# Attention and FFN on one core: strided value tiles of 128 rows, strided pairs first, masks loaded in two parts

## The chip, the core and the metric

The kernel runs on one core of one Trainium2 chip. The metric is the device time of one execution in microseconds (us), the median of several. The engines named below are PE (TensorE matmul; PEld is its weight load), DVE (VectorE), ACT (ScalarE), POOL (GpSimd) and SP (SyncE, which here only issues DMAs). The core has 16 DMA engines.

## What is computed

Eight batches of eight heads, 576 tokens, head size 64. Heads 0 to 3 see a local window of the last 32 tokens, heads 4 to 7 see every 32nd token back from their own. The result goes, token by token, through an FFN of 512 to 2048 to 512.

```python
def reference(q, k, v, w_in, w_out):
    scores = q @ k.T / sqrt(64)                  # per batch and head
    rel = i - j
    mask = (0 <= rel < 32) if head < 4 else (rel >= 0 and i % 32 == j % 32)
    attn = softmax(where(mask, scores, -1e9)) @ v
    x = attn.transpose(0, 2, 1, 3).reshape(4608, 512)
    h = x @ w_in
    return (h * sigmoid(1.702 * h)) @ w_out
```

## The kernel before, in words

The host lays the inputs out in the order in which the kernel reads them (`_layout`, from L707). Attention is cut into units, called pairs in the code. A *local* pair ("l") holds four blocks of 64 queries with 96 keys each, for four heads: its queries and keys come in one tile of 128 rows (`qk <- lqk`, 576 KB), its values in one of 96 rows (`v <- lv`, 384 KB). A *strided* pair ("s") holds a third of a batch's 32 residue classes: `qk <- sqk`, 452 KB in 128 rows, and its values `v <- sv`, in 118 rows of 2 KB (236 KB; `QB + NB` is 64 + 54: two groups of 54 keys, the second from row 64 on). There are 18 local and 24 strided pairs.

`_pairs` (L59) lists the pairs in the order of the work: `ahead`, those done before the FFN starts, and `windows`, those woven into the FFN of later token groups. A token group is 384 tokens; the FFN of a group takes 16 steps (one for each 128 of the 2048 hidden units), `ffn1` making a hidden tile and `ffn2` adding it, two steps later, to three output tiles. Nine pairs are ahead: before the change l, l, s, s, s, s, l, s, s. They are numbered 0 to 8 below; the stretch in which they are done is called the lead.

The lead is a loop written out by hand (L607 to L635). In iteration i, for a pair each: PE makes the scores of pair i+1 (`scores`: masks are added by a matmul of the mask rows with an identity matrix, both from the tile `masks_sb`, then 32 small matmuls); SP loads the qk of pair i+3; DVE and POOL scale pair i-1 by the reciprocal of its sums; DVE fetches pair i-2's transposed weights from PSUM (`fetch_pt`); DVE takes the row maxima of pair i+1; ACT does the exponentials of pair i (eight instructions); PE makes the value products of pair i-2 (`values`, the matmuls "a <- pt, v"); ACT casts them to the FFN's high part (`xhl`, `xhs`), DVE later makes the low part; SP loads the values of pair i; ACT and DVE do one of the three passes that split a 128-wide slice of the FFN weights (`weigh`, from tiles `raw`) into high and low parts; PE transposes pair i-1 (`turn_pr`, "t"). Each engine keeps to the order in which the program is written.

Two things tie SP's queue to the rest. The qk and v tiles have two buffers each, so `load_qk(i+3)` waits for the scores of pair i+1, and `load_v(i)` for the value products of pair i-2; what stands behind a waiting load on SP waits too. And a DMA that shares its completion semaphore with an earlier one waits until that has landed; eight semaphores go round.

After the lead come the FFN steps, in which PE is kept busy by the `ffn1` and `ffn2` matmuls ("h" and "o"); the strided and local pairs that remain are done beside them, with the mask added on DVE instead. The lead's end and the first steps overlap: the value products of pairs 6, 7 and 8 stand before, in and after steps 0 to 2 on PE, and the weight slices for steps 2 and on are loaded and split while the steps run.

The tile `masks_sb` is 672 columns wide: five local mask blocks of 96, the strided one of 54 at `MASK_S` (480), the identity at `MASK_I` (544). One DMA (L154) loads it first of all. `geom` (L171) picks the mask of a pair, `scores` (L193) the identity.

Of the kernel before, what the change touches and what calls it, by code (L numbers as in the profile page):

```python
# [18 lines left out]
P = 128  # L19
B, H, S, D = 8, 8, 576, 64  # L20
# [4 lines left out]
QB = 64  # L25
KB = QB + STRIDE
RB = 3
NB = RB * NPOS
U = 2
# [3 lines left out]
NR = (12, 10, 10)  # L33
# [1 line left out]
QW = (U * 2 * QB, U * (NB + QB))  # L35
KW = (U * (KB + QB), U * 2 * NB)
QKW = tuple(2 * (a + b) for a, b in zip(QW, KW))
MASK_S = 5 * KB
MASK_I = 544
MASKS = MASK_I + P  # L40
G = 384
NG = B * S // G
NF = DFF // P
# [4 lines left out]
HEADS = 4  # L48
# [10 lines left out]
def _pairs():  # L59

    def strided(b):
        return [("s", b, c) for c in range(len(NR))]

    def local(j):
        return [("l", i, 0) for i in range(-(-j * G // LT), -(-(j + 1) * G // LT))]

    def weave(a, b):
        return [u for i in range(max(len(a), len(b))) for u in a[i : i + 1] + b[i : i + 1]]  # L70

    first = {}
    for b in range(B):
        first.setdefault(b * S // G, []).extend(strided(b))
    ahead = local(0) + first[0]
    windows = [weave(first.get(j + 1, []), local(j + 1)) for j in range(NG - 1)] + [[]]
    ahead += windows[0]
    windows[0] = []
    return ahead + [u for w in windows for u in w], windows, len(ahead)
# [3 lines left out]
def attn_ffn(ctx, tc, lqk, sqk, lv, sv, w_in, w_out, masks, ident, out):  # L83
# [11 lines left out]
    def bank(name):  # L95
        tag, n = ("s", 2) if name[0] == "s" else ("x", 6)
        return psum.tile([P, 512], F32, tag=tag, name=name, bufs=n)
# [8 lines left out]
    class InOrder:  # L106
# [17 lines left out]
    vector, scalar, gpsimd, sync = (  # L124
        InOrder(e, strict) for e in (nc.vector, nc.scalar, nc.gpsimd, nc.sync)
    )
# [3 lines left out]
    qks, vts, banks, nmaxs, exps = {}, {}, {}, {}, {}  # L130

    def load_qk(p):
        if p < len(pairs) and p not in qks:
            kind, a, c = pairs[p]
            src, n = (lqk[a], QKW[0]) if kind == "l" else (sqk[a * len(NR) + c], QKW[1])
            qks[p] = st4([P, QKW[0]], F32, f"qk_{p}")
            for i in (slice(0, n // 2), slice(n // 2, n)) if p == 0 else (slice(0, n),):
                sync.dma_start(out=qks[p][:, i], in_=src[:, i])

    def load_v(p):  # L140
        if p < len(pairs) and p not in vts:
            kind, a, c = pairs[p]
            vts[p] = io.tile([P, 2 * U * HEADS * D], F32, tag="v", name=f"v_{p}", bufs=2)
            if kind == "l":
                sync.dma_start(out=vts[p][:KB], in_=lv[a])
            else:
                n = U * HEADS * D
                sync.dma_start(out=vts[p][: QB + NB, :n], in_=sv[a * len(NR) + c])

    warm = const.tile([P, 1], F32, name="warm")  # L150
    vector.memset(warm, 0.0)
    scalar.activation(warm, warm, AF.Exp)
    masks_sb = const.tile([P, MASKS], BF16, name="masks_sb")
    sync.dma_start(out=masks_sb, in_=masks)  # L154
    load_qk(0)
    zeros = const.tile([P, P], BF16, name="zeros")
    vector.memset(zeros, 0.0)
# [4 lines left out]
    first = [[bank(f"{x}{j}") for j in range(2)] for x in "sut"]  # L162
# [8 lines left out]
    def geom(p):  # L171

        kind, a, _ = pairs[p]
        if kind == "s":
            m = masks_sb[:, MASK_S : MASK_S + NB]
            return NB, m.unsqueeze(1).broadcast_to([P, 2 * U, NB])
        begins = [i for i in range(2 * U) if (2 * U * a + i) % (S // QB) == 0]
        if not begins:
            m = masks_sb[:, KB : 2 * KB]
            return KB, m.unsqueeze(1).broadcast_to([P, 2 * U, KB])  # L180
        at = (0, 2, 3, 1)[begins[0]] * KB
        m = masks_sb[:, at : at + U * KB]
        return KB, m.unsqueeze(1).broadcast_to([P, 2, U * KB])

# [8 lines left out]
    def scores(p):  # L193

        nk, mask = geom(p)
        onto = p < n0
        sps = first[p % 2] if onto else [bank(f"s{j}_{p}") for j in range(2)]
        n = mask.shape[1]
        if onto:
            for sp in sps:  # L200
                matmul(
                    sp[:, : 2 * U * nk].rearrange("p (a n) -> p a n", a=n),
                    lhsT=masks_sb[:, MASK_I:], rhs=mask, start=True, stop=False,
                )
        for h in range(2):
            for u in range(U):
                i = h * U + u
                for g in range(2):
                    for j in range(2):
                        q, k = operands(p, slice(j * D, (j + 1) * D), h, u, g)  # L210
                        matmul(
                            sps[j][g * QB : (g + 1) * QB, i * nk : (i + 1) * nk],
                            lhsT=q,
                            rhs=k,
                            start=not onto,
                            stop=not onto or i == 2 * U - 1,
                        )
        banks[p] = sps
# [169 lines left out]
    def load_w(f):  # L388

        if f >= NF:  # L390
            return
        raw = raws[f] = w_tile([P, 2, DM, 2], U32, f"raw_{f}")
        for m in range(2):
            sync.dma_start(out=raw[:, m], in_=(w_in, w_out)[m][f])
# [190 lines left out]
    for _ in range(6):  # L585
        matmul(
            first[2][0].rearrange("p (a n) -> p a n", a=4), lhsT=zeros,
            rhs=zeros.unsqueeze(1).broadcast_to([P, 4, P]), start=True, stop=True,
# [2 lines left out]
    maxima(0)  # L591
    load_qk(2)
    load_v(1)
    load_w(0)
    halfway, valued = {}, {}

# [41 lines left out]
    at = {}  # L638
# [3 lines left out]
    p = n0  # L642
# [10 lines left out]
    begins = {}  # L653
    for p in range(n0, len(pairs)):
        begins[max(turn.get(p - AHEAD, -1) + 1, turn[p] - SOON)] = p
    for s in range(len(steps) + LAG):
# [3 lines left out]
        p, q, r = due.get(s), due.get(s - 1), begins.get(s)  # L660
# [46 lines left out]
def _layout(q, k, v, w_in, w_out):  # L707
    hl = H // 2
    pad = np.zeros((B, hl, STRIDE, D), np.float32)
    kp, vp = (np.concatenate([pad, x[:, :hl]], axis=2) for x in (k, v))  # L710
    nb = S // QB

    lqk = np.zeros((NP, 2, D, 2, QKW[0] // 2), np.float32)
    lv = np.zeros((NP, KB, 2 * U, HEADS, D), np.float32)
    for i in range(NP):
        for m in range(2 * U):
            b, n = divmod(2 * U * i + m, nb)
            u, g = divmod(m, 2)
            rows = q[b, :hl, n * QB : (n + 1) * QB]
            keys = kp[b, :, n * QB : n * QB + KB]  # L720
            at = u * 2 * QB + g * QB
            lqk[i, :, :, :, at : at + QB] = rows.reshape(2, 2, QB, D).transpose(1, 3, 0, 2)
            at = QW[0] + u * (KB + QB) + g * QB
            skip = STRIDE if g and not n else 0
            lqk[i, :, :, :, at + skip : at + KB] = keys[:, skip:].reshape(
                2, 2, KB - skip, D
            ).transpose(1, 3, 0, 2)
            lv[i, :, m] = vp[b, :, n * QB : n * QB + KB].transpose(1, 0, 2)

    ns = B * len(NR)  # L730
    sqk = np.zeros((ns, 2, D, 2, QKW[1] // 2), np.float32)
    sv = np.zeros((ns, QB + NB, U, HEADS, D), np.float32)
    for i in range(ns):
        b, c = divmod(i, len(NR))
        for m in range(2 * U):
            g, u = divmod(m, U)
            r0, r1 = R0[c] + RB * m, R0[c] + min(RB * (m + 1), NR[c])
            n = (r1 - r0) * NPOS
            x = [
                y[b, hl:].reshape(hl, NPOS, STRIDE, D)[:, :, r0:r1].transpose(0, 2, 1, 3).reshape(hl, n, D)  # L740
                for y in (q, k, v)
            ]
            at = u * (NB + QB) + g * NB
            sqk[i, :, :, :, at : at + n] = x[0].reshape(2, 2, n, D).transpose(1, 3, 0, 2)
            at = QW[1] + u * 2 * NB + g * NB
            sqk[i, :, :, :, at : at + n] = x[1].reshape(2, 2, n, D).transpose(1, 3, 0, 2)
            sv[i, g * QB : g * QB + n, u] = x[2].transpose(1, 0, 2)
    lqk, sqk = (x.reshape(len(x), P, -1) for x in (lqk, sqk))
    lv, sv = (x.reshape(*x.shape[:2], -1) for x in (lv, sv))

    wi = w_in.reshape(NC, P, NF, P).transpose(2, 1, 0, 3).reshape(NF, P, DM)
    wo = w_out.reshape(NF, P, DM)
    wi, wo = (np.ascontiguousarray(x).view(np.uint64) for x in (wi, wo))
    return lqk, sqk, lv, sv, wi, wo


def _masks():
    import ml_dtypes

    m = np.full((P, MASKS), NEG, ml_dtypes.bfloat16)  # L760
    i, g = np.arange(P)[:, None] % QB, np.arange(P)[:, None] // QB
    k = np.arange(KB)[None, :] - STRIDE
    ok = (i - k >= 0) & (i - k < STRIDE)
    for n, begins in enumerate((0, None, 1, None, 0)):
        some = ok if begins is None else ok & ((g != begins) | (k >= 0))
        m[:, n * KB : (n + 1) * KB][some] = 0.0
    k = np.arange(NB)[None, :]
    ok = (i // NPOS == k // NPOS) & (i >= k)
    m[:, MASK_S : MASK_S + NB][ok] = 0.0
    m[:, MASK_I:] = np.eye(P)  # L770
    return m


# [24 lines left out]
```

## Time and profile before

| | |
|---|---|
| three runs | 947.21, 945.47, 946.59 us; median 946.59 |
| the profiled execution | 947.53 us |
| its span, first to last instruction | 945.7 us |
| PE busy | 913.9 us, 97% of the span |
| DVE, ACT, POOL busy | 476.1, 380.6, 53.0 us |
| moved by DMA | 62.08 MB, 66 GB/s over the span |
| mean granted clock of TensorE | 0.98 of full speed |

The profile is one execution on the chip. Its page gives the busy time of each engine; a table by stretches gives it for any piece of the span, with PE's granted clock (1.00 is full speed), the share of the 16 DMA engines that was busy and the GB/s they moved. The time line gives instructions in order: start, duration, engine, line, operation, out<-in, and in brackets the idle time ahead of the first one and what ended it. All engines go through one helper, so every row has the same line, L116, and rows are told apart by their tiles. The chain of waits follows the work that ended last back from the end. A DMA's row on SP is its issue, not its transfer.

### The profile page before, as it was taken

What the parts mean: (1) busy time and instruction counts of PE and PEld (TensorE: products, weight loads), DVE (VectorE), ACT (ScalarE), POOL (GpSimd) and SP (SyncE); (2) the same over time, 40 slices, a digit from 0 to 9 for tenths busy, and PEclk for the clock granted to TensorE, in tenths of its full rate; (3) what the DMA queues carried; (4) which work ended last, traced back from release to release, by engine and by line L of the source; (5) the groups of instructions that cost most, each with busy time, mean ns of one, the idle gap of its engine ahead of it and who ended that gap; (6) DMA issues with size and microseconds to landing.
All of it is one profiled execution on the core that took longest, in us unless ns stands there. A gap on an engine that the chain in (4) does not pass through costs nothing.

```text
span 945.7 us, 16069 instructions
## 1 busy us (share of the span) xinstructions
PE 913.9 (97%) x6432; PEld 806.6 (85%) x6432; DVE 476.1 (50%) x986; ACT 380.6 (40%) x1193; POOL 53.0 (6%) x50
## 2 busy tenths in 40 slices
PE   6569999999999999999999999999999999999998
PEld 4457888888888888888888888888888888898997
DVE  3648656565454663443655564453446565322322
ACT  5649755243433442423444333332433443222221
POOL 3100001010000100000000000000000010000000
PEclk6779999999999999999999999999999999999999
DMA  8659202112112111101212120110201310000000
GB/s 262 197 164 348 97 1 90 60 41 96 35 42 84 53 53 51 45 1 64 72 50 72 52 57 34 53 38 20 80 31 43 105 29 1 34 1 1 34 1 33
DMA packets 21242, 62.08 MB, mean 66 GB/s; under 512 B 2144, under 2 KB 2400, under 8 KB 21168
## 3 DMA queue, kind: packets, MB, share of 16 engines
q1 hardware_dynamic: 21168, 61.06, 19.7%
q8 instruction: 50, 0.82, 0.4%
q14 instruction: 24, 0.20, 0.1%
HBM read 51.62 MB, written 9.44 MB: 65 GB/s over the span
## 4 chain that ended last, share of the span: by engine, by line
PE 92%; DMA 7%; DVE 0%; issue 0%; SPq 0%; ACT 0%; DVEq 0%; ACTq 0%
PE o L116 43%; PE h L116 41%; PE a L116 4%; DMA v<-sv 4%; PE s L116 3%; DMA raw<-w_out 1%; DMA qk<-sqk 1%; DMA qk<-lqk 1%; PE u L116 0%; PE t L116 0%; SPq L116 0%; ACT raw L116 0%; DVE raw L116 0%; DVE w L116 0%; DVE out L116 0%
## 5 line engine op out<-in xcount | busy, mean ns | idle before, releaser
L116 PE MATMUL o<-w,gh 128*128 128x512 f32 x1152 | 307.6, 398 | 0.0
L116 PEld LDWEIGHTS o<-w,gh 128*128 128x128 f32 x1152 | 211.1, 187 | 39.0 <-ACT gh L116 0.4
L116 PE MATMUL h<-xhl,w 128*128 128x384 f32 x768 | 229.7, 339 | 2.0 <-DVE w L116 1.4
L116 PE MATMUL h<-xhs,w 128*128 128x384 f32 x768 | 227.2, 336 | 0.0
L116 DVE SCALAR_TENSOR_TENSOR g<-g,h 128x384 f32<-128x384 f32 x192 | 106.1, 553 | 225.2 <-ACT g L116 224.6
L116 ACT ACTIVATE g<-h 128x384 f32<-128x384 f32 x192 | 93.7, 488 | 264.3 <-PE h L116 188.1
L116 PE MATMUL o<-w,gl 128*128 128x512 f32 x576 | 169.6, 395 | 0.0
L116 ACT CAST gh<-g 128x384 fp32r<-128x384 f32 x192 | 98.8, 514 | 155.2 <-DVE g L116 155.1
L116 PEld LDWEIGHTS h<-xhl,w 128*128 128x128 f32 x768 | 142.3, 188 | 12.2 <-DVE w L116 2.3
L116 DVE TENSOR_TENSOR gl<-g,gh 128x384 fp32r<-128x384 f32 x192 | 112.0, 583 | 77.6 <-ACT gh L116 76.1
L116 PEld LDWEIGHTS h<-xhs,w 128*128 128x128 f32 x768 | 141.9, 188 | 0.1
L116 PEld LDWEIGHTS o<-w,gl 128*128 128x128 f32 x576 | 107.8, 187 | 26.6
L116 PE MATMUL h<-xll,w 128*128 128x384 f32 x384 | 129.6, 338 | 0.0
L116 PE MATMUL h<-xls,w 128*128 128x384 f32 x384 | 128.7, 335 | 0.0
L116 ACT ACTIVATE pr<-pr,nmax 128x54 f32<-128x54 f32 (+1 forms) x264 | 90.3, 344 | 87.6 <-DVE nmax L116 84.6
L116 POOL TENSOR_TENSOR pr<-pr,rinv 128x432 f32<-128x432 f32 (+1 forms) x42 | 49.6, 1182 | 734.5 <-DVE rinv L116 728.0
L116 PEld LDWEIGHTS h<-xll,w 128*128 128x128 f32 x384 | 72.4, 189 | 8.8
L116 PEld LDWEIGHTS h<-xls,w 128*128 128x128 f32 x384 | 72.4, 188 | 0.0
L116 DVE STREAM_TRANSPOSE pt_l<-pr 32x256 f32<-32x256 f32 x120 | 52.2, 435 | 2.3 <-POOL pr L116 0.8
L116 DVE STREAM_TRANSPOSE pt_s<-pr 32x256 f32<-32x256 f32 x108 | 47.1, 436 | 9.5 <-POOL pr L116 8.0
L116 ACT ACTIVATION_READ_ACCUMULATOR pr<-pr,nmax 128x1 f32 x264 | 49.4, 187 | 0.0
L116 PE MATMUL a<-pt_s,v 118*64 118x108 f32 x384 | 25.3, 278 | 13.8 <-DMA v<-sv 12.2
(55 smaller groups left out, 462.3 us busy)
## 6 DMA issues: line engine op xcount, KB each, us to landing
qk<-sqk SPq DMA_DIRECT2D x24, 452.0 KB
qk<-lqk SPq DMA_DIRECT2D x17, 576.0 KB
out<-out SPq DMA_DIRECT2D x36, 256.0 KB
raw<-w_in SPq DMA_DIRECT2D x16, 512.0 KB
raw<-w_out SPq DMA_DIRECT2D x16, 512.0 KB
v<-lv SPq DMA_DIRECT2D x18, 384.0 KB
v<-sv SPq DMA_DIRECT2D x24, 236.0 KB
qk<-lqk SPq DMA_DIRECT2D x2, 288.0 KB
```

The costliest lines, as they stand in the source:

```text
L116: ins = call(*args, **kw)
```

## The change

Three edits, all to what stands around the lead.

*Values in 128 rows.* The host pads the strided values from 118 to 128 rows with zeros, and `load_v` loads all 128 (256 KB). The value products still read 118 rows.

*Strided pairs first.* In `_pairs`, the first group's strided pairs go ahead of its local ones: the nine pairs are now s, s, s, l, l, s, l, s, s. The pairs from the sixth on are the same as before.

*Masks in two parts.* The tile's columns are laid out anew: the strided mask, the identity, then the local blocks from `MASK_L` (192) on. The first DMA loads 192 columns (48 KB), a second one, issued behind the values of pair 1, the other 480 (120 KB).

```diff
-MASK_S = 5 * KB
-MASK_I = 544
-MASKS = MASK_I + P
+MASK_I = 64
+MASK_L = MASK_I + P
+MASKS = MASK_L + 5 * KB
...
-    ahead = local(0) + first[0]
+    ahead = first[0] + local(0)
...
-                sync.dma_start(out=vts[p][: QB + NB, :n], in_=sv[a * len(NR) + c])
+                sync.dma_start(out=vts[p][:, :n], in_=sv[a * len(NR) + c])
...
-    sync.dma_start(out=masks_sb, in_=masks)
+    sync.dma_start(out=masks_sb[:, :MASK_L], in_=masks[:, :MASK_L])
...
-            m = masks_sb[:, MASK_S : MASK_S + NB]
+            m = masks_sb[:, :NB]
...
-            m = masks_sb[:, KB : 2 * KB]
+            m = masks_sb[:, MASK_L + KB : MASK_L + 2 * KB]
...
-        at = (0, 2, 3, 1)[begins[0]] * KB
+        at = MASK_L + (0, 2, 3, 1)[begins[0]] * KB
...
-                    lhsT=masks_sb[:, MASK_I:], rhs=mask, start=True, stop=False,
+                    lhsT=masks_sb[:, MASK_I:MASK_L], rhs=mask, start=True, stop=False,
...
     load_qk(2)
     load_v(1)
+    sync.dma_start(out=masks_sb[:, MASK_L:], in_=masks[:, MASK_L:])
     load_w(0)
...
-    sv = np.zeros((ns, QB + NB, U, HEADS, D), np.float32)
+    sv = np.zeros((ns, P, U, HEADS, D), np.float32)
```

How this moves instructions is read from the built programs, engine by engine. First SP at the start of the program, before: the masks, then the loads of pairs 0 to 4 (`qk_0`, `v_0` and so on are the tiles of pair 0; `raw_0` is the first slice of the FFN weights).

```order
L116 DMA masks_sb_82<-masks 128x672
L116 DMA qk_0_84<-lqk 128x576 x2
L116 DMA qk_1_107<-lqk 128x1152
L116 DMA v_0_109<-lv 96x1024
L116 DMA ident_sb_111<-ident 128x128
L116 DMA qk_2_141<-sqk 128x904
L116 DMA v_1_143<-lv 96x1024
L116 DMA raw_0_145<-w_in 128x1024
L116 DMA raw_0_145<-w_out 128x1024
L116 DMA qk_3_166<-sqk 128x904
L116 DMA qk_4_199<-sqk 128x904
```

The same place now:

```order
L116 DMA masks_sb_82<-masks 128x192
L116 DMA qk_0_84<-sqk 128x452 x2
L116 DMA qk_1_107<-sqk 128x904
L116 DMA v_0_109<-sv 128x512
L116 DMA ident_sb_111<-ident 128x128
L116 DMA qk_2_141<-sqk 128x904
L116 DMA v_1_143<-sv 128x512
L116 DMA masks_sb_82<-masks 128x480
L116 DMA raw_0_146<-w_in 128x1024
L116 DMA raw_0_146<-w_out 128x1024
L116 DMA qk_3_167<-lqk 128x1152
L116 DMA qk_4_200<-lqk 128x1152
```

The order of the loads is the same but for the second mask load, ahead of the first weights; the smaller strided tiles now stand in front, and the larger local ones behind the weights.

Next SP in the middle of the lead, the loads of pairs 5 to 8 and the values of pairs 2 to 5, before:

```order
L116 DMA qk_5_249<-sqk 128x904
L116 DMA v_2_288<-sv 118x512
L116 DMA qk_6_319<-lqk 128x1152
L116 DMA v_3_359<-sv 118x512
L116 DMA raw_2_363<-w_in 128x1024
L116 DMA raw_2_363<-w_out 128x1024
L116 DMA qk_7_393<-sqk 128x904
L116 DMA v_4_430<-sv 118x512
L116 DMA qk_8_463<-sqk 128x904
L116 DMA v_5_496<-sv 118x512
```

The same place now:

```order
L116 DMA qk_5_250<-sqk 128x904
L116 DMA v_2_285<-sv 128x512
L116 DMA qk_6_317<-lqk 128x1152
L116 DMA v_3_350<-lv 96x1024
L116 DMA raw_2_354<-w_in 128x1024
L116 DMA raw_2_354<-w_out 128x1024
L116 DMA qk_7_384<-sqk 128x904
L116 DMA v_4_417<-lv 96x1024
L116 DMA qk_8_450<-sqk 128x904
L116 DMA v_5_491<-sv 128x512
```

Pairs 3 and 4 are local now, so two of the four value loads come from `lv`, 96 rows of 4 KB, and the strided ones have 128 rows.

Last ACT in iterations 2 to 4, before: exponentials ("pr, ssum <- ..., nmax", four heads a row), casts of value products, and passes over the weights.

```order
L116 CAST xhl_0_286<-a0_97 128x2x256
L116 ACTIVATE raw_1_218<-raw_1_218 128x1024
L116 ACTIVATE pr_1_100,ssum_3_332<-u0_93,nmax_3_257 128x54 x4
L116 ACTIVATE pr_1_100,ssum_3_332<-u1_94,nmax_3_257 128x54 x4
L116 CAST xhl_0_286<-a1_98 128x2x128
L116 CAST xhl_1_357<-a1_98 128x2x128
L116 ACTIVATE raw_1_218<-raw_1_218 128x1024
L116 ACTIVATE pr_0_99,ssum_4_409<-s0_91,nmax_4_328 128x54 x4
L116 ACTIVATE pr_0_99,ssum_4_409<-s1_92,nmax_4_328 128x54 x4
```

The same place now:

```order
L116 CAST xhs_0_281<-a0_97 128x24x12
L116 CAST xhs_1_283<-a0_97 128x2x6x12
L116 ACTIVATE raw_1_219<-raw_1_219 128x1024
L116 ACTIVATE pr_1_100,ssum_3_333<-u0_93,nmax_3_260 128x96 x4
L116 ACTIVATE pr_1_100,ssum_3_333<-u1_94,nmax_3_260 128x96 x4
L116 CAST xhs_0_281<-a1_98 128x24x10
L116 CAST xhs_1_283<-a1_98 128x2x6x10
L116 ACTIVATE raw_1_219<-raw_1_219 128x1024
L116 ACTIVATE pr_0_99,ssum_4_400<-s0_91,nmax_4_329 128x96 x4
L116 ACTIVATE pr_0_99,ssum_4_400<-s1_92,nmax_4_329 128x96 x4
```

The kinds of work keep their order on ACT; the longer local exponentials (96 columns a head instead of 54) move from pairs 0 and 1 to pairs 3 and 4.

More of the change, by code (lines that the diff above doesn't have):

```diff
@@ L765, in _masks @@
         some = ok if begins is None else ok & ((g != begins) | (k >= 0))
-        m[:, n * KB : (n + 1) * KB][some] = 0.0
+        m[:, MASK_L + n * KB : MASK_L + (n + 1) * KB][some] = 0.0
     k = np.arange(NB)[None, :]
     ok = (i // NPOS == k // NPOS) & (i >= k)
-    m[:, MASK_S : MASK_S + NB][ok] = 0.0
-    m[:, MASK_I:] = np.eye(P)
+    m[:, :NB][ok] = 0.0
+    m[:, MASK_I:MASK_L] = np.eye(P)
     return m
```

## The prediction

> **What bounds the kernel now.** I read the page first, then a table by stretches of the span, then the chain of waits of the first 140 us, then the waits engine by engine there, and the time lines of that stretch. The page's first lines:
>
> ```profile
> span 945.7 us, 16069 instructions
> ...
> PE 913.9 (97%) x6432; PEld 806.6 (85%) x6432; DVE 476.1 (50%) x986; ACT 380.6 (40%) x1193; POOL 53.0 (6%) x50
> ```
>
> PE is busy 97% of the span, so what can be won on other engines lies where PE idles. The table by stretches (length, busy time of each engine with its instructions, PE's granted clock, share of the 16 DMA engines, GB/s) says where that is:
>
> ```profile
> 0.00:88.78 88.78, 61.11 (x666) 48.66 (x666) 48.58 (x114) 54.77 (x192) 13.27 (x17) 0.79 0.73 235
> 100.00:900.00 800.00, 799.96 (x5509) 711.06 (x5508) 406.61 (x841) 304.98 (x968) 39.75 (x33) 1.00 0.15 47
> ```
>
> From 100 to 900 us PE idles 0.04 us: nothing on another engine or queue matters there, and the 18 strided value loads of that part are hidden. In the first 88.78 us PE is busy 61.11 us, at a mean clock of 0.79. All that this change can move is in those 88.78 us: the lead, nine pairs done before the first FFN step, and the first FFN steps. The chain there (start, us, what):
>
> ```profile
> 26.49 10.14 DMA v<-sv
> ...
> 38.50 15.25 DMA v<-sv
> ...
> 55.63 14.05 DMA v<-sv
> ...
> 71.65 11.10 DMA raw<-w_out
> ...
> 92.91 2.10 PE h L116 x12
> ```
>
> Three strided value loads hold it for 39.4 us. Who stood still meanwhile, in the waits of ACT from 32 to 66 us and of PE from 32 to 77 us (total, times, longest):
>
> ```profile
> ACT xhs L116 <- PE a L116: 12.7, 3, 4.6
> ACT xhl L116 <- PE a L116: 4.8, 1, 4.8
> ```
> ```profile
> PE a L116 <- DMA v<-sv: 12.2, 4, 4.1
> PE a L116 <- DMA v<-lv: 3.1, 1, 3.1
> ```
>
> PE's value products wait for v, and ACT's casts wait for the products: one stall, seen on two engines.
>
> **Why these loads are slow.** Five rows of the table by stretches: a strided load with nothing beside it, whole and its middle; a local value load alone; a stretch of the lead; a stretch of weight loads.
>
> ```profile
> 762.03:769.10 7.07, 7.07 (x63) 6.19 (x64) 5.13 (x12) 2.42 (x8) 0.00 (x0) 1.00 0.12 37
> 764.00:768.50 4.50, 4.50 (x24) 4.00 (x23) 3.34 (x8) 1.84 (x5) 0.00 (x0) 1.00 0.12 47
> 776.51:780.00 3.49, 3.49 (x45) 2.96 (x46) 1.71 (x4) 1.90 (x5) 0.00 (x0) 1.00 0.48 117
> 56.00:62.00 6.00, 3.40 (x13) 2.83 (x11) 3.37 (x7) 3.54 (x18) 0.91 (x1) 0.72 0.13 53
> 82.00:94.00 12.00, 11.27 (x56) 9.55 (x55) 9.39 (x13) 11.29 (x15) 0.00 (x0) 1.00 1.01 398
> ```
>
> A strided load of 118 rows alone keeps 0.12 of 16 engines busy, so two, at 47 GB/s: its 236 KB (241,664 B) take 5.1 us of those two and 7.07 us in all. A local one of 96 rows and 384 KB is done in 3.49 us. At 398 GB/s, the rate on all engines, 256 KB need 0.66 us. From 56 to 62 us the lead shows the same picture: 0.13 of the engines, 53 GB/s, while PE waits for v. That wait is even for a local load, issued 15 us earlier, because its share of the two slow engines stands behind the strided ones (SP's row, then PE's rows of the first 100 us that I need here and below):
>
> ```profile
> 47.52 0.33 SPq L116 DMA_DIRECT2D v<-lv  x1
> ```
> ```profile
> 25.30 1.15 PE L116 MATMUL a<-pt_l,v 96*64 96x64 f32 x32
> ...
> 62.47 1.79 PE L116 MATMUL a<-pt_l,v 96*64 96x64 f32 x32 [3.07 <-DMA v<-lv]
> 64.18 0.69 PE L116 MATMUL h<-xhs,w 128*128 128x384 f32 x1
> ...
> 66.22 1.03 PE L116 MATMUL t<-ident_sb,pr 128*54 128x128 f32 x8
> ...
> 69.81 0.96 PE L116 MATMUL a<-pt_s,v 118*64 118x108 f32 x16 [0.48 <-DMA v<-sv]
> ...
> 76.65 1.66 PE L116 MATMUL o<-w,gh 128*128 128x512 f32 x6
> ...
> 84.08 0.61 PE L116 MATMUL h<-xhl,w 128*128 128x384 f32 x2 [0.52 <-DVE w L116]
> ...
> 92.74 0.34 PE L116 MATMUL h<-xhl,w 128*128 128x384 f32 x1
> ```
>
> **The change part by part.**
>
> *128 rows.* If 128 rows spread over all 16 engines as the other 128-row loads do, one such load takes between 2.0 us (7.07 less its 5.1 of transfer, and no transfer) and 3.5 us (the larger local one); I take 2.6, 2.0 and the 0.66. Each of the six loads in the lead frees 5.1 - 0.66 = 4.4 us of the two engines' queue, 27 us in sum, more than all the stalls below. What is late next decides. I cost the lead in four pieces.
>
> A, from the exponentials of pair 5 (ACT, 32.30) to the products of pair 6 (62.47). This piece, a stretch in which v is not yet late, and three more for the transfer rate:
>
> ```profile
> 32.30:62.47 30.17, 15.36 (x179) 12.38 (x168) 14.92 (x40) 14.41 (x74) 4.64 (x5) 0.72 0.59 179
> 25.00:35.00 10.00, 6.34 (x148) 5.23 (x144) 9.23 (x28) 9.21 (x48) 1.82 (x2) 0.99 0.72 231
> 2.00:22.80 20.80, 13.10 (x185) 9.14 (x183) 7.34 (x21) 10.57 (x53) 4.87 (x5) 0.65 0.91 292
> 6.00:14.00 8.00, 3.69 (x70) 2.88 (x70) 2.77 (x10) 5.16 (x32) 1.47 (x1) 0.63 1.01 259
> 22.80:48.00 25.20, 15.71 (x249) 12.72 (x248) 15.53 (x43) 16.07 (x77) 5.12 (x5) 0.77 0.61 194
> ```
>
> The piece holds 14.92 us of DVE work, 14.41 of ACT and 15.36 of PE (at a clock of 0.72, so less when PE runs on). Without the waits DVE and ACT become the pace. They depend on each other in every iteration, and in the free stretch from 25 to 35 us DVE filled 9.23 of 10 us. So 14.92 / 0.92 = 16.2 us, and A gains 30.17 - 16.2 = 14.0. Its upper end is no slack at all beside DVE, 15.3. Its lower end is the transfers: everything queued up to pair 6's values is 6 x 452 + 4 x 576 KB of qk, 4 x 256 + 3 x 384 KB of v, 5 MB of weights, 232 KB of masks and identity, 12.85 MB. At 292 GB/s from 2 us on that lands at 46.0, before the 48.5 at which A wants it; at 259, the slow patch of the lead, at 51.6, and A gains 10.9.
>
> B, from there to the first output product: 76.65 - 62.47 = 14.2 us now. The wait for pair 7 (0.48) goes. The products run at part clock, 1.79 us against the 1.15 of the same products at 25.30, and so does the half step from 64.18 to 66.22, 2.0 us against half of the chain's 2.10; the chain over tanh, cast and split behind them stays. I take 1.0, between 0.5 (the wait alone) and 2.1 (0.48 + 0.64 + 1.0).
>
> C, the first four output and hidden groups, 76.65 to 92.74: 16.1 us. At the chain's 2.10 us a group, seven groups need 14.7; some 1.3 us are lost to late weights (the 11.10 us of raw<-w_out in the chain is one such load behind two strided ones, on the same two engines). I take 1.0, between 0 and 1.3.
>
> *Strided pairs first.* D, the front up to 32.30. Pair 3's load ends the front's wait, and it becomes a local one, 124 KB larger:
>
> ```profile
> 10.22 8.85 DMA qk<-sqk
> ```
> ```profile
> 40.23 0.33 ACT L116 ACTIVATE pr<-s,nmax 128x96 f32<-128x96 f32 x1
> ...
> 42.45 0.37 ACT L116 ACTIVATE pr<-s,nmax 128x96 f32<-128x96 f32 x1
> ...
> 48.96 0.30 ACT L116 ACTIVATE pr<-u,nmax 128x54 f32<-128x54 f32 x1
> ...
> 50.93 0.35 ACT L116 ACTIVATE pr<-u,nmax 128x54 f32<-128x54 f32 x1
> ```
>
> Ahead of it now stand two qk loads smaller by 124 KB each and two v loads smaller by 128 KB each: 504 KB less, and with its own 124 KB more 380 KB less, 1.3 us at 292 GB/s. Against that, two local pairs now do their exponentials in the part where ACT sets the pace: 42.82 - 40.23 = 2.59 us against 51.28 - 48.96 = 2.32, twice 0.27, and I allow 0.4 for their longer scores on PE. D gains 1.3 - 0.5 - 0.4 = 0.4, between -1 (the shorter queue is worth nothing) and 2.4 (PE's 0.4 doesn't count, and half of the 2.8 us goes that the patch from 6 to 14 us, at 259 GB/s, costs against 398).
>
> *Masks apart.* The first part shrinks from 168 to 48 KB, the second, 120 KB, is one more issue on SP, behind pair 1's values and ahead of the first weights. PE used the masks before qk came:
>
> ```profile
> 3.13 0.15 PEld L116 LDWEIGHTS <-masks_sb 128*128 128x128 bf16 x1 [0.28 <-DMA masks_sb<-masks]
> ...
> 4.33 0.53 PEld L116 LDWEIGHTS s<-qk 64*64 64x64 f32 x16 [0.62 <-DMA qk<-lqk]
> ```
>
> So the smaller first part only shortens the queue ahead of qk (0.4 us at 292 GB/s, not all of which survives the later waits). The second part is first read by pair 3's scores, which waited until 19 us for qk; it lands some 9 us ahead of them. I set both at nothing; without that cover pair 3 would wait for 120 KB, 0.4 us. The extra issue costs SP 0.4 us once, ahead of loads that queue for longer. It also waits for the first part to land; the first weights and pair 3's qk stand behind it on SP. But it comes after pair 2's qk, which waits for pair 0's scores, and these begin at 4.33, when the first part has been read.
>
> The rest, 88.78 to the end, is PE's own work and stays. Sum: 14.0 + 1.0 + 1.0 + 0.4 = 16.4 us. The profiled execution took 947.53 us for its span of 945.7; it becomes 931.1. The median of the three runs, 946.59, is 0.94 lower: 930.2.
>
> **The rivals.**
>
> First, the engines were not the point: the transfers are simply slow while everything is loaded, and at the 194 GB/s of 22.8 to 48 us pair 6's values land late whoever carries them. With 6.07 MB moved by 22.8 us the other 6.78 MB need 35 us: 57.7. A gains 4.8, B 0.5, C 0.5, D 0.4: 6.2, so 940.4. For it: weights of 5 MB go through the same lead. Against it: 0.61 of the engines busy at that rate, not all. Chance 0.11.
>
> Second, the change doesn't do what it says: a value load's time doesn't depend on its rows, or 128 rows still go to two engines. Then the lead keeps six slow loads, only D moves (-1 to 2.4), and the time lies between 944 and 948. Against it: 128-row qk and weight loads keep all engines busy (1.01), the 118-row load two. Chance 0.06, of which a third faster, half the same.
>
> The Trainium skill speaks for both sides here. Its page "DMA: Bandwidth & Descriptors", section "Anatomy of one DMA", fits a transfer by its bytes alone, about 2.0 us plus bytes over 436 GB/s; by that estimate the load takes 2.55 us with 118 rows and 2.60 with 128, and piece A would gain nothing. The trace's 7.07 us denies that. The same page's section "Why a DMA increments its semaphore by 16 and not by 1" has a transfer run on the largest number up to 16 that divides its slowest dimension: 2 for 118, 16 for 128 and for 96. The rows with 118 and 96 agree; 128 rows of v no run has shown yet.
>
> Third, on the other side: slower. The strided loads ran on two engines and left the other fourteen to qk and weights. Spread, each adds 0.66 us to all of them, six in the lead 4.0 us. If what ends the lead's waits are those fourteen engines, nothing is won and 4.0 us lost: 950.6. It decides from the point where the fourteen are still busy when PE is released. Against it: 56 to 62 us, where they lie idle and PE waits. Chance 0.04.
>
> **How the numbers follow.** The forecast has 0.77, the rest (0.02) is unknown. Its own range: all upper ends, 15.3 + 2.1 + 1.3 + 2.4 = 21.1, give 925.5; all lower ends, 10.9 + 0.5 + 0 - 1 = 10.4, give 936.2. To leave out no more than 2 in 10 it reaches up to the first rival: 925 to 940. Under 0.2% (1.9 us) is no change here, about what measuring this kernel tells apart. Faster: 0.77 + 0.11 + 0.02 + 0.01 = 0.91; same 0.04; slower 0.05.
>
> **What would show it.** Right: no strided v load in the chain; a strided load alone takes about 2.6 us instead of 7.07; pair 6's products begin near 48 us, the first output product near 62 (PE's first "o" row, 76.65 now); from there on PE gap-free. Wrong: ACT still waiting over 2 us an iteration for products (the rate of transfer, first rival), an isolated strided load still at 0.12 of the engines (second), or DMA share near 1 while PE waits (third).

## The result, and the profile after

The changed kernel takes 929.07 us (median of four runs, 928.27 to 932.00) against 946.03 for the kernel before in the same comparison: a ratio of 0.9826, 95% interval 0.9801 to 0.9851. The forecast was 930.2 us, 925 to 940. The profiled execution took 929.46 us. Its page, first lines:

```profile
span 927.7 us, 16071 instructions
...
PE 908.0 (98%) x6432; PEld 801.7 (86%) x6432; DVE 475.3 (51%) x986; ACT 379.6 (41%) x1193; POOL 53.0 (6%) x50
```

The span is 18.0 us shorter. The table by stretches of the changed kernel (length; busy PE, PEld, DVE, ACT, POOL; clock; share of the 16 DMA engines; GB/s): the three pieces A, B and C between the same marks as in the prediction, then a fixed stretch that was quoted for the kernel before, then a strided load with nothing beside it.

```profile
29.40:46.31 16.91, 10.78 (x178) 8.96 (x179) 14.20 (x37) 14.44 (x73) 5.29 (x5) 0.90 1.02 332
46.31:59.98 13.67, 12.30 (x110) 10.49 (x111) 8.53 (x17) 9.11 (x13) 0.10 (x1) 0.88 0.65 223
59.98:74.80 14.82, 14.82 (x75) 13.16 (x74) 12.68 (x18) 14.76 (x22) 0.00 (x0) 1.00 1.03 374
22.80:48.00 25.20, 18.42 (x321) 15.03 (x318) 20.50 (x56) 21.18 (x104) 7.13 (x6) 0.91 0.94 302
744.01:747.02 3.01, 3.01 (x43) 2.55 (x44) 2.34 (x7) 1.43 (x4) 0.00 (x0) 1.00 0.34 93
```

From 22.8 to 48 us the DMA engines are 0.94 busy at 302 GB/s, where they were 0.61 busy at 194. An isolated strided load takes 3.01 us instead of 7.07. The marks come from the time lines of ACT and PE (start, duration, idle before and what ended it): the first exponentials of pair 5 on ACT; on PE the scores of pair 3, the value products of pairs 4 to 7, the first output product, and the group that answers to the 92.74 of the kernel before.

```profile
29.40 0.41 ACT L116 ACTIVATE pr<-u,nmax 128x54 f32<-128x54 f32 x1
```
```profile
16.58 1.56 PE L116 MATMUL u<-qk 64*64 64x96 f32 x32 [2.98 <-DMA qk<-lqk]
...
35.42 1.15 PE L116 MATMUL a<-pt_l,v 96*64 96x64 f32 x32 [0.87 <-DMA v<-lv]
...
39.64 1.16 PE L116 MATMUL a<-pt_s,v 118*64 118x108 f32 x16
...
46.31 1.51 PE L116 MATMUL a<-pt_l,v 96*64 96x64 f32 x32 [3.46 <-DMA v<-lv]
...
53.13 0.96 PE L116 MATMUL a<-pt_s,v 118*64 118x108 f32 x16
...
59.98 1.67 PE L116 MATMUL o<-w,gh 128*128 128x512 f32 x6
...
74.80 0.34 PE L116 MATMUL h<-xhl,w 128*128 128x384 f32 x1
```

No strided product waits for its values here. Of the waits for values, one of 3.46 us is left, for pair 6's local values, and a short one of 0.87 us for pair 4's. The chain of waits shows the same: its four transfers (start, us, what) are

```profile
2.11 5.64 DMA qk<-sqk
8.57 7.97 DMA qk<-lqk
...
27.11 8.18 DMA v<-lv
...
36.60 9.57 DMA v<-lv
```

None is a strided value load; there were 39.4 us of these in the chain. The last one, pair 6's values, lands at 36.60 + 9.57 = 46.17, and SP's time line shows what stands ahead of it in the queue:

```profile
31.71 0.43 SPq L116 DMA_DIRECT2D raw<-w_in  x1
32.19 0.42 SPq L116 DMA_DIRECT2D raw<-w_out  x1
32.66 0.43 SPq L116 DMA_DIRECT2D raw<-w_in  x1
33.13 0.87 SPq L116 DMA_DIRECT2D raw<-w_out  x1
34.63 0.33 SPq L116 DMA_DIRECT2D qk<-lqk  x1
36.60 0.33 SPq L116 DMA_DIRECT2D v<-lv  x1
```

These are 2 MB of weights, in the tiles raw_3 and raw_4. With the DMA share at 1.02 in piece A, the lead now seems to be held by how much is in the queue, where two engines of 16 held it before; the runs with one weight load out of the way, below, test this.

### The profile page after: what moved, and what is told of

Same layout as the page of the kernel before. It is cut to its first block, busy times and chain, and to the rows that moved or that the text cites. A ratio compares the mean times of both kernels' runs of the same rounds, so it can differ in the third digit from the quotient of the medians.

```text
span 927.7 us, 16071 instructions
## 1 busy us (share of the span) xinstructions
PE 908.0 (98%) x6432; PEld 801.7 (86%) x6432; DVE 475.3 (51%) x986; ACT 379.6 (41%) x1193; POOL 53.0 (6%) x50
## 4 chain that ended last, share of the span: by engine, by line
PE 95%; DMA 3%; DVE 1%; ACT 0%; issue 0%; SPq 0%; DVEq 0%
PE o L116 44%; PE h L116 43%; PE a L116 4%; PE s L116 3%; DMA v<-lv 2%; DMA qk<-lqk 1%; DMA qk<-sqk 1%; DVE pt_s L116 0%; PE u L116 0%; DVE nmax L116 0%; DVE w L116 0%; DVE raw L116 0%; SPq L116 0%; PE t L116 0%; ACT w L116 0%
## 5 line engine op out<-in xcount | busy, mean ns | idle before, releaser
L116 DVE TENSOR_SCALAR rinv<-ssum 128x8 f32<-128x8 f32 x42 | 7.1, 169 | 57.8 <-ACT pr L116 57.7
```

The source lines that it names most:

```text
L116: ins = call(*args, **kw)
```

## The experiments

Theory: two DMA engines carry a 118-row load, everything queued behind it waits for these two, and 128 rows end that. Rivals: it is the order of the pairs (smaller tiles first); it is the bytes or the masks. All runs stand in one table, with the marks of each profiled execution. "Ratio" is to the kernel before, measured beside it, with its 95% interval; the last column is span less the start of the first output product.

| kernel | median us | ratio | pair 5 exp. | pair 6 products | first output | rest |
|---|---|---|---|---|---|---|
| before | 946.03 | 1 | 32.30 | 62.47 | 76.65 | 869.0 |
| changed | 929.07 | 0.9826 (0.9801 to 0.9851) | 29.40 | 46.31 | 59.98 | 867.7 |
| changed, again | 930.40 | 0.9828 (0.9813 to 0.9843) | 29.84 | 48.82 | 62.53 | 867.7 |
| rows alone | 931.07 | 0.9842 (0.9827 to 0.9856) | 30.92 | 46.38 | 61.49 | 867.7 |
| rows alone, again | 931.89 | 0.9848 (0.9830 to 0.9865) | 29.76 | 47.48 | 61.63 | 867.8 |
| 118 rows, rest changed | 946.65 | 1.0005 (0.9996 to 1.0014) | 38.30 | 61.76 | 76.34 | 868.7 |
| masks in one load | 930.20 | 0.9828 (0.9815 to 0.9842) | 29.01 | 46.15 | 60.44 | 867.7 |
| 120 rows | 931.23 | 0.9847 (0.9831 to 0.9864) | 29.28 | 47.29 | 61.05 | 867.8 |
| 124 rows | 939.78 | 0.9929 (0.9916 to 0.9941) | 34.18 | 56.16 | 70.30 | 867.7 |
| 112 and 6 rows | 932.69 | 0.9856 (0.9842 to 0.9869) | 29.54 | 48.36 | 62.24 | 868.6 |
| raw_4 late | 927.27 | 0.9800 (0.9786 to 0.9813) | 29.11 | 44.90 | 57.22 | 867.8 |
| raw_4 late, again | 926.39 | 0.9787 (0.9765 to 0.9809) | 29.47 | 44.27 | 56.45 | 867.8 |
| rows alone, raw_4 late | 927.38 | 0.9795 (0.9780 to 0.9811) | 31.62 | 45.34 | 57.92 | 867.7 |
| three raw buffers | 927.74 | 0.9803 (0.9790 to 0.9817) | 29.51 | 43.36 | 57.01 | 867.7 |

The last column is the plainest reading: where no 118-row load is left and values come in one load, the rest of the program takes 867.7 to 867.8 us whatever was done ahead of it. The time is settled when the first output product starts.

**Rows alone.**

```
-                sync.dma_start(out=vts[p][: QB + NB, :n], in_=sv[a * len(NR) + c])
+                sync.dma_start(out=vts[p][:, :n], in_=sv[a * len(NR) + c])
...
-    sv = np.zeros((ns, QB + NB, U, HEADS, D), np.float32)
+    sv = np.zeros((ns, P, U, HEADS, D), np.float32)
```

> The kernel before, with nothing changed but the rows of the strided values: 128 instead of 118 (old order of the pairs, masks in one load). Theory (the two-engine queue of the 118-row loads is what costs; 128 rows take all 16 engines): pieces A, B and C move as they did in the changed kernel (13.3 + 0.5 + 1.3 = 15.1 us) and the front, D, doesn't (exponentials of pair 5 on ACT still at 32.3 +- 0.5 instead of 29.4): 930.5 to 933 us; an isolated strided load 2.6 to 3.2 us. First rival (the order of the pairs, with its smaller tiles first, gains most): 938 or more. Second rival (the rows gain D too, since the front is held by two-engine loads): 929 +- 0.7.

It took 931.07 us, as the theory has it. Rows of PE, the products of pair 2 (the first strided one in this order) and of pair 6:

```profile
26.91 0.40 PE L116 MATMUL a<-pt_s,v 118*64 118x108 f32 x2 [0.28 <-DVE pt_s L116]
27.70 0.95 PE L116 MATMUL a<-pt_s,v 118*64 118x108 f32 x14 [0.40 <-DVE pt_s L116]
...
46.38 1.98 PE L116 MATMUL a<-pt_l,v 96*64 96x64 f32 x32 [3.29 <-DMA v<-lv]
```

The kernel before has pair 2's products, too, on its time line:

```profile
29.81 0.93 PE L116 MATMUL a<-pt_s,v 118*64 118x108 f32 x15 [1.57 <-DVE nmax L116]
```

These products come 2 to 3 us earlier with 128 rows, but most of that is not the rows' doing. Pair 3's scores begin at 17.22 here and at 19.12 in the kernel before (PE), and the first strided values are issued only after them, at 20.28 here and at 22.18 before (SP's time line):

```profile
17.22 1.12 PE L116 MATMUL u<-qk 64*64 64x54 f32 x32 [1.05 <-DMA qk<-sqk]
```
```profile
19.12 1.11 PE L116 MATMUL u<-qk 64*64 64x54 f32 x32 [3.38 <-DMA qk<-sqk]
```

The programs do the same up to there, so these 1.9 us are a difference between two executions. They also cover the move of the front's mark (30.92 against 32.30), which was more than the 0.5 us allowed. A fairer pair is the run with 128 rows and raw_4 late, further below, whose scores of pair 3 begin at 19.28, as late as before; its products of pair 2 come at 27.92 without a wait:

```profile
19.28 1.11 PE L116 MATMUL u<-qk 64*64 64x54 f32 x32 [3.15 <-DMA qk<-sqk]
...
27.92 1.46 PE L116 MATMUL a<-pt_s,v 118*64 118x108 f32 x16
```

That is 1.9 us ahead of the 29.81 of the kernel before. So with 118 rows the first strided load is most likely late already there, ahead of where the prediction let the stalls begin, though the profile puts that wait of 1.57 us down to DVE.

**118 rows, the rest of the change kept.** The same two lines, the other way round, in the changed kernel.

> The changed kernel with 118 rows of strided values again (new order and split masks kept). Theory: the slow loads are back, and three of them now stand in the front, ahead of pair 3's scores and values: A, B and C are lost, and D as well: 943 to 950 us, the isolated strided load 7 us at 0.12 of the DMA engines, strided v loads in the chain of the lead. Rival (the order gains): 938 or less.

946.65 us, ratio 1.0005: without the rows, the order and the split masks together are worth nothing. PE's waits of the first 100 us (total, times, longest), the chain's transfers, and the isolated load:

```profile
PE a L116 <- DMA v<-sv: 8.5, 2, 5.7
PE a L116 <- DMA v<-lv: 4.5, 2, 3.9
PE u L116 <- DMA masks_sb<-masks: 3.8, 1, 3.8
```
```profile
26.82 8.78 DMA v<-sv
36.86 7.50 DMA v<-lv
45.68 15.95 DMA v<-lv
```
```profile
761.32:768.66 7.34, 7.34 (x65) 6.46 (x66) 5.26 (x13) 2.54 (x9) 0.00 (x0) 1.00 0.11 35
```

The front is 6.0 us later than in the kernel before (38.30 against 32.30), since strided loads now stand ahead of all else; the piece from there to pair 6 is 6.7 us shorter. The worst sufferers are other loads: a local one takes 15.95 us, and the second part of the masks, set at nothing in the prediction, is waited for 3.8 us.

**120 rows and 124 rows.** `vts[p][:120, :n]` and `vts[p][:124, :n]` with the host's array to match, in the changed kernel.

> The changed kernel with 120 rows of strided values instead of 128. If a load runs on the largest number up to 16 that divides its rows, 120 gives 15 engines: the same time as 128 rows, 928.5 to 930, isolated load 2.6 to 3.3 us. Rival (only the full 128 rows are spread, anything less goes to two engines or few): 943 to 950, with 7 us for the isolated load.

> The changed kernel with 124 rows of strided values: 248 KB, fewer bytes than with 128 rows, but the largest number up to 16 that divides 124 is 4. By the divisor: four engines, an isolated load takes 2.0 us and half of the 5.1 us of two engines and a little more, 4.5 to 5 us at about 0.25 of the DMA engines, and the lead loses a part of what 128 rows win: 932 to 938. By bytes: 929. If anything under 128 that isn't a multiple of 8 or 16 falls to two engines: 943 to 950.

120 rows took 931.23 us, above the range given, with an interval that overlaps that of 128 rows; 124 rows, with more bytes than 120, took 939.78, also a little above the range of the divisor rule. The isolated load with 120 rows, then with 124, whole and its middle:

```profile
745.10:748.27 3.17, 3.17 (x44) 2.71 (x45) 2.49 (x7) 1.43 (x4) 0.00 (x0) 1.00 0.31 83
```
```profile
754.32:759.22 4.90, 4.90 (x54) 4.44 (x55) 3.60 (x9) 1.94 (x5) 0.00 (x0) 1.00 0.18 55
755.80:758.50 2.70, 2.70 (x15) 2.43 (x15) 2.01 (x7) 1.42 (x4) 0.00 (x0) 1.00 0.22 83
```

With 118 rows 0.12 of 16 engines were busy, which is 1.9; with 124 rows it is 0.22, or 3.5. How many engines a load used can also be counted. The DMA view of the same stretches, each with this one load in it, gives the packets for 118 rows (the kernel before), 124, 120 and 128:

```profile
DMA packets 121, 0.26 MB, mean 37 GB/s; under 512 B 2, under 2 KB 2, under 8 KB 120
```
```profile
DMA packets 129, 0.27 MB, mean 55 GB/s; under 512 B 4, under 2 KB 4, under 8 KB 128
```
```profile
DMA packets 136, 0.26 MB, mean 83 GB/s; under 512 B 15, under 2 KB 15, under 8 KB 135
```
```profile
DMA packets 145, 0.28 MB, mean 93 GB/s; under 512 B 16, under 2 KB 16, under 8 KB 144
```

Next to one packet a row there are 2, 4, 15 and 16 small ones (and one larger one of another queue). Read as one for each engine, they agree with the busy shares: two engines, four, 15 and 16.

The times fit one line in the bytes for each engine: 118 KB an engine take 7.07 us (7.34 in the run with 118 rows above) and 62 KB 4.90. That is 0.039 to 0.044 us a KB (23 to 26 GB/s an engine) and 2.2 to 2.5 us of fixed time, both estimates from these three rows; 16 KB an engine then give 2.9 to 3.1, measured 3.01 (128 rows) and 3.17 (120). What counts is neither the rows nor the bytes as such but the number of engines that they are spread over, and that is the largest divisor up to 16 of the row count. The Trainium skill states this rule ("DMA: Bandwidth & Descriptors", "Why a DMA increments its semaphore by 16 and not by 1"). These traces agree with it, for 118, 124, 120 and 128 rows.

**The same 118 rows in two loads**, in the changed kernel:

```
-                sync.dma_start(out=vts[p][:, :n], in_=sv[a * len(NR) + c])
+                sync.dma_start(out=vts[p][:112, :n], in_=sv[a * len(NR) + c, :112])
+                sync.dma_start(out=vts[p][112:118, :n], in_=sv[a * len(NR) + c, 112:118])
```

> The changed kernel with the 118 rows loaded as two loads, 112 rows and 6 rows, so that the same 118 rows arrive with no padding, but the first load divides by 16 and the second by 6. Theory (engines, not rows or bytes): 928.5 to 930.5, DMA share of the isolated load far over 0.12, no strided v load in the chain; the second issue costs SP some 0.3 us a pair, hidden. Rival (it is the odd row count as such, the 118th row of the tile, that is slow): 940 or more.

932.69 us: padding isn't needed for most of the gain, and the isolated loads, both parts together, take 2.89 us at 0.33 of the engines:

```profile
746.27:749.16 2.89, 2.89 (x43) 2.43 (x44) 2.21 (x7) 1.43 (x4) 0.00 (x0) 1.00 0.33 89
```

The second load had been expected to be hidden, and the time is above the range given: by the ratios 2.6 to 2.8 us more than the changed kernel's two measurements, give or take 1.9 and 2.7. Against the expectation, its chain holds a strided load again, one of 5.93 us in the front, and pair 6's wait is the longest of all kernels whose loads are spread:

```profile
2.58 5.93 DMA v<-sv
...
36.67 11.55 DMA v<-lv
```
```profile
48.36 1.98 PE L116 MATMUL a<-pt_l,v 96*64 96x64 f32 x32 [7.19 <-DMA v<-lv]
```

Still, its first output product, at 62.24, lies between those of the changed kernel's two profiled executions (59.98 and 62.53). The 0.9 us behind it (868.6 against 867.7) lie at the very end: from the end of DVE's last instruction to the end of the span it is 4.3 us here and 3.4 in the changed kernel. What the second load costs in the lead is therefore not settled.

**Masks in one load**, ahead of pair 0's qk as before, in the changed kernel:

```
-    sync.dma_start(out=masks_sb[:, :MASK_L], in_=masks[:, :MASK_L])
+    sync.dma_start(out=masks_sb, in_=masks)
...
-    sync.dma_start(out=masks_sb[:, MASK_L:], in_=masks[:, MASK_L:])
```

> The changed kernel with the masks in one load again, ahead of pair 0's qk (168 KB instead of 48). Theory (masks apart are worth nothing, as forecast): 929 to 929.6, exponentials of pair 5 at 29.4 to 29.8. Rival (the front's gain, 2.9 us where 0.4 was forecast, is the masks'): 930.5 to 932, exponentials of pair 5 at 31 or later.

930.20 us, 0.9828 against the changed kernel's 0.9826: the split is worth nothing that these runs can tell. The front's mark (29.01) is no later, so the rival falls too.

**One weight load out of the way.** In the changed kernel, raw_4 is issued behind pair 6's values:

```
-            if f + RAWB < NF - 1:
+            if f and f + RAWB < NF - 1:
...
             load_v(i)
+            if i == 6:
+                load_w(RAWB)
```

> The changed kernel with one weight load (raw_4, 1 MB of w_in and w_out) issued behind pair 6's values instead of ahead of them. In the changed kernel it lands at 42.4 us and is first cast at 55.6, while PE waits 3.46 us for pair 6's values, which land at 46.2 behind it. Theory (the lead is now bound by transfers in the order of issue): 1 MB at 300 GB/s is 3.5 us, the wait goes, and then ACT and DVE set the pace (14.44 and 14.20 us of work in the 16.91 us from 29.40): 1.0 to 2.7 us less, 926.4 to 928.1. Rival (the total of the bytes counts, the next load in the queue is then late by as much): 929 +- 0.6.

927.27 us, inside the theory's range and the best so far. Pair 6's products wait 0.18 us where it was 3.46, and the first output product comes at 57.22:

```profile
44.90 1.28 PE L116 MATMUL a<-pt_l,v 96*64 96x64 f32 x32 [0.18 <-DMA v<-lv]
...
57.22 1.67 PE L116 MATMUL o<-w,gh 128*128 128x512 f32 x6
```

**Three raw buffers** (`RAWB = 3` for 4) take the same megabyte out of the queue with one line.

> The changed kernel with three buffers for raw weights instead of four, so that every weight load goes out later by one step and 1 MB less stands in the queue ahead of pair 6's values. Theory (transfers in the order of issue): the 3.46 us wait for pair 6's values shrinks as in the run with raw_4 late, 926.4 to 928.1, if the weights still come in time. Rival: weights come late at the first output products (DMA share is 1.03 from 60 to 75 us), and the lead's gain is lost there again: 929 to 934.

927.74 us, inside the theory's range. Pair 6's products begin at 43.36, after a wait of 2.0 us, and the weights still come in time (rest 867.7).

```profile
43.36 1.97 PE L116 MATMUL a<-pt_l,v 96*64 96x64 f32 x32 [2.00 <-DMA v<-lv]
```

**Order of the pairs by raw_4, four kernels on one chip.** What was left open is how much the order gives, since the front's gain was 2.90 us where 0.4 was forecast. The changed kernel and the one with raw_4 late are run again, beside the rows alone, and the rows alone with the same raw_4 edit.

> The changed kernel once more, first of four kernels on one chip: new order of the pairs, raw_4 early. It says how far two executions differ: exponentials of pair 5 on ACT at 29.0 to 29.6, pair 6's products at 46 to 47, 928 to 930 us.

> The kernel before with 128 rows alone once more: old order, raw_4 early. Exponentials of pair 5 at 30.9 to 31.5 (it was 30.92; the old order is that much later in the front), but pair 6's products again at 46 to 47, because their values land when the transfers ahead of them are done, and these are the same. Theory (what the new order wins in the front is lost again at pair 6's values): no more than 1 us above the changed kernel. Rival (the order's 1.4 us of the front reach the end): 1.3 to 2.5 us above it.

> The changed kernel with raw_4 behind pair 6's values once more: new order, raw_4 late. 1.0 to 2.7 us below the changed kernel of this call, with no wait of over 1 us for v in the lead.

> The kernel before with 128 rows, and raw_4 behind pair 6's values: old order, raw_4 late. Where transfers no longer hold pair 6, ACT and DVE run through, so that the order's gain in the front should now reach the end. Theory: 1.2 to 2.0 us above the changed kernel with raw_4 late, and 0.5 to 2.0 below the rows alone with raw_4 early. Rival (the order is worth nothing in any case, its front gain is scatter of one execution): within 0.7 us of the changed kernel with raw_4 late.

With raw_4 early they take 930.40 us (new order) and 931.89 (old), with raw_4 late 926.39 and 927.38. By the ratios, which all four have to the same runs of the kernel before, raw_4 late wins 0.0041 (give or take 0.0027, the two half intervals combined) in the new order and 0.0053 (0.0023) in the old: 3.9 and 5.0 us, more than the 2.7 expected at most (the first run of raw_4 late, 0.9800, lies 2.5 us below the changed kernel's 0.9826). The order wins 0.0020 (0.0023) and 0.0008 (0.0027): 1.9 and 0.8 us, neither to be told from zero, and neither the theory nor the rival of these two runs is settled. The front marks of the two runs in the old order, rows alone and with raw_4 late:

```profile
29.76 0.48 ACT L116 ACTIVATE pr<-u,nmax 128x54 f32<-128x54 f32 x1
```
```profile
31.62 0.42 ACT L116 ACTIVATE pr<-u,nmax 128x54 f32<-128x54 f32 x1
```

One order, the same loads up to there, and 1.9 us between two executions, of which 1.8 are there already when pair 3's scores begin (17.49 and 19.28): a single profile doesn't settle a difference of that size in the front. Nor does it further on: the first output products of the changed kernel's two executions lie 2.6 us apart (59.98 and 62.53). And an early front need not help: the run that was at 29.76 waits longest,

```profile
47.48 1.97 PE L116 MATMUL a<-pt_l,v 96*64 96x64 f32 x32 [5.47 <-DMA v<-lv]
```

while the one at 31.62 has pair 6's products at 45.34. With raw_4 late in the new order again, one wait of 2.54 us for pair 6's values was left in the profiled execution, against the expectation of none over 1 us, and the run was no slower for it:

```profile
44.27 1.15 PE L116 MATMUL a<-pt_l,v 96*64 96x64 f32 x32 [2.54 <-DMA v<-lv]
```

## Why the prediction was right, point by point

*128 rows spread the load over all engines.* Right, and shown: undone alone, the gain is gone (1.0005), made alone, it is nearly all there (0.9842 and 0.9848). The load takes 3.0 us where 2.6 was taken, within its bounds: the fixed part comes out at 2.2 to 2.5 us and not at 2.0. The fit by bytes alone that the prediction took from the Trainium skill ("DMA: Bandwidth & Descriptors", "Anatomy of one DMA") is given there for DMAs issued by POOL (GpSimd), and these loads are issued by SP. So the 7.07 us show that it does not carry over to them, not that it is wrong.

*A, 14.0 us forecast.* 30.17 - 16.91 = 13.26. The size was near, the limit named for it was not. The step that failed is "Without the waits DVE and ACT become the pace": the piece still ends in a wait of 3.46 us for transfers, the case set as the lower end. The prediction had the transfers right: by its sum pair 6's values land at 46.0, and they landed at 46.17. It set DVE's pace behind them, at 48.5; with the front 2.9 us earlier even that pace, 29.40 + 16.2 = 45.6, would have come first. And the pace itself was set too slow: taking one megabyte out of the queue won 3.9 and 5.0 us, and it brought the piece to 44.90 - 29.11 = 15.79 and 44.27 - 29.47 = 14.80 us in the new order and to 45.34 - 31.62 = 13.72 in the old one, all below the 16.2. So the 14.92 us of DVE work that lay in the piece need not all be done there; in those 13.72 us DVE was busy for 12.46:

```profile
31.62:45.34 13.72, 10.86 (x146) 8.45 (x147) 12.46 (x37) 12.85 (x65) 3.89 (x4) 0.88 0.97 323
```

*B, 1.0 forecast.* 14.18 - 13.67 = 0.51, the lower end: pair 7's wait went, but the clock is still only 0.88 in the piece, and pair 6's products take 1.51 us, not the 1.15 that the same products took at 25.30 in the kernel before.

*C, 1.0 forecast.* 16.09 - 14.82 = 1.27: the late weights went, and PE has no gap there. The last column of the table says the same, 869.0 against 867.7.

*D, 0.4 forecast.* 32.30 - 29.40 = 2.90, over its upper end: the mis-sized term. (That end was given as 2.4; its own terms, 0.4 + 0.4 + 1.4, add up to 2.2.) The time lines of all runs take D apart at the point where pair 3's scores begin, which is where the prediction saw the front's wait end. The means, in us:

| kernels | to pair 3's scores | from there to pair 5's exp. | sum |
|---|---|---|---|
| new order, spread loads (eight executions) | 16.17 (15.37 to 16.91) | 13.23 | 29.40 |
| old order, 128 rows (three) | 18.00 (17.22 to 19.28) | 12.77 | 30.77 |
| before (one) | 19.12 | 13.18 | 32.30 |

So the shorter queue ahead of pair 3 gave 1.8 us where 1.3 was taken, and the longer work behind it cost 0.5 where 0.9 was taken: 1.4 us for the order, as a mean of executions of which those in the old order lie almost 2 apart. The other 1.5 lie between the old order with 128 rows and the kernel before. Of these, 1.1 stand ahead of pair 3's scores, where no strided value load has been issued yet: they are not the rows' doing, and no more than the scatter of the three. The other 0.4 stand where the first strided load was late; they can be the rows, but are within the scatter. That the order's 1.4 us in the front reach the end is not shown: the three independent comparisons of the whole kernel (rows alone against the changed kernel with its masks in one load, and the two pairs of the last four kernels: 1.3, 1.9 and 0.8 us by the ratios) all have the same sign, and each has an interval that includes zero. Weighted by their intervals they give 1.4 us, give or take 1.2: likely, but a narrow case.

*The sum.* 16.4 us were forecast and 18.0 came, in the profiled executions. The sum is closer than its terms, and that is luck: A and B gave 1.2 us less than forecast, C and D 2.8 more, and more than one of D's 2.9 us is not an effect of the change.

*Masks, 0.* Right as long as the loads are spread. The cover is needed, though: with two-engine loads ahead of it, the second part was waited for 3.8 us, where the prediction had put 0.4 for a cover gone.

*The rivals.* Slow transfers (194 GB/s) fell: 302 GB/s now. "The change doesn't do it" fell with the isolated load. The slower side, spread loads that burden the fourteen others, has a grain of truth: the sign that the prediction set for it, a DMA share near 1 while PE waits, did appear in A (1.02). But the gain there is far larger than the price.

The version that beats both kernels is the changed one with raw_4 late, 927.27 and 926.39 us, 0.9800 and 0.9787 of the kernel before.

## What to carry to other kernels

Read the DMA share of a transfer that runs alone: 0.12 of 16 engines is two engines, and then not only that transfer is late but the loads queued behind it as well; the count of small packets says the same. A row count whose largest divisor up to 16 is small, as 2 is for 118, is worth padding. When such a load is gone, look at once at what stands in the queue ahead of the next late tile: here moving a megabyte of weights behind it was worth another 2.5 to 5 us. Before a gain of one or two us in a start-up phase is believed, profile the same kernel twice.

## What was not expected of the hardware

By the lines above, the fixed part of an isolated load is 2.2 to 2.5 us and one engine moves 23 to 26 GB/s (estimates, from 7.07 and 7.34 us at 118 KB an engine and 4.90 at 62). In the DMA view the number of engines of a load can be counted: 2, 4, 15 and 16 packets under 512 B for 118, 124, 120 and 128 rows. A local load of 384 KB that takes 3.49 us alone took 15.95 us in the chain beside loads on two engines. And the same front differs by almost 2 us between executions (29.76 to 31.62).
